# Causal masks on POOL in two instructions of two heads each, with a new instruction order, in a kernel of attention and token MLP

## The chip, the cores and the metric

One core of one Trainium2 chip. The metric is the device time of one execution in microseconds (us). The kernel before takes 174.0 us (median of 3 runs, 173.86 to 174.17). All times below are of fast runs, medians and ranges too; the slow are named and left out.

## The reference, cut to what matters

The output is a gated sum of two branches over X (2048 x 448): attention in 4 segments of 512 tokens with 16 heads of 28, causal inside a segment, with a memory matrix carried from segment to segment; and an MLP across tokens.

```python
mask = (ar[:, None] < ar[None, :]) * -1000000000.0       # causal, inside a segment
for s in range(N):                                        # N = 4 segments
    logits = einsum('bhqd,bhkd->bhqk', qs, ks) * scale + mask
    p = softmax(logits)
    a_dot = einsum('bhqk,bhkd->bhqd', p, vs)
    num = einsum('bhld,bhde->bhle', phi(qs), M)           # memory of earlier segments
    den = einsum('bhld,bhd->bhl', phi(qs), z)[..., None] + 1e-06
    outs.append(g * num / den + (1 - g) * a_dot)
    M = M + einsum('bhld,bhle->bhde', phi(ks), vs)
    z = z + einsum('bhld->bhd', phi(ks))
a = concat(outs) @ wo
b = gelu(layernorm(x)^T @ w1 + b1) @ w2 + b2
out = gate * a + (1 - gate) * b
```

## The kernel before

Work is recorded as named operations with what they read and write. A table ORDER then fixes, by hand or search, the sequence on each of the five engines; waits are derived from the reads and writes. The exponentials of one score fill (128 keys x 4 heads x 512 columns) go to one buffer `g`; POOL then zeroes the part above the diagonal in each 128-column block of it, all four heads at once:

```python
op("ACT", lambda e: e.activation(pslot(g), ps[:, 0:4, :], ACT.Exp, scale=SCALE), reads=R_bank[0:4],
   writes=[g.res], take=g, name=f"exp{p}_{f}", ...)
for x, j, c0, w in FILLS[f]:
    op("POOL", lambda e, c0=c0: e.affine_select(pslot(g)[:, :, c0 : c0 + 128], pslot(g)[:, :, c0 : c0 + 128],
                                                pattern=[[0, 4], [1, 128]], compare_op=ALU.is_ge, fill=0.0,
                                                base=0, channel_multiplier=-1),
       reads=[g.res], writes=[g.res], name=f"mask{p}_{f}_{j}", ...)
```

`g.res` is one tracked resource: whoever reads or writes any part of the buffer waits for the last writer of any part.

A full matmul (128 x 128 weights) may be issued whole or as four matmuls of 32 columns that run side by side. The second form is chosen where PE is already working in 32-column tiles, to save a change of form (name `mst`: the memory product, 64 matmuls of 32 x 32; `pv`: probabilities times V):

```python
def mm(e, out, w, x, split, **kw):
    if not split:
        return e.matmul(out, w, x, ...)
    for q in range(0, 128, 32):
        last = e.matmul(out[q : q + 32], w[:, q : q + 32], x, ...)
    return last
```

The loads of W1, W2 and Wo, the transposes of X and of the keys are all issued from one engine, SP, in the sequence of its row of ORDER. W1 comes in seven loads of 1 MB into a ring of three slots.

The softmax here doesn't subtract the row's maximum and nothing guards it: scores larger than these inputs give would overflow.

## Time and profile before

| | before |
|---|---|
| time, median of 3 | 174.0 us |
| span of the profiled execution | 170.9 us (that execution took 172.65 us) |
| PE / DVE / ACT / POOL busy | 166.1 / 144.2 / 127.0 / 68.6 us |
| masks | 64, 637 ns median |

PE is busy nearly throughout, so the time is that of PE: useful columns, about 0.1 us at each change of form, and halts. The lines that carry it stand in the prediction. One thing to keep in view: the profiled execution, at 172.65 us, was faster than each of the three timed ones, by 1.2 us and more.

### The profile page before, as it was taken

How to read it: one execution, taken by the hardware profiler on the slowest of the kernel's cores; microseconds unless marked ns; L12 is line 12 of the kernel's file. 1: busy time of each engine (PE TensorE's matmuls, PEld its weight loads, DVE VectorE, ACT ScalarE, POOL GpSimd, SP SyncE). 2: the span in 40 equal slices, each digit the busy share in tenths (PEclk: the TensorE clock that was granted, in tenths of full speed). 3: DMA queues.
4: the chain of work that ended last, by engine and by line, in shares of the span. 5: the costliest groups of instructions: out<-in, count | busy, mean ns of one | idle time of the engine just before them, and what ended most of it. 6: DMA issues, size and time to landing. Idle time of an engine off the chain costs nothing.

```text
span 170.9 us, 4757 instructions
## 1 busy us (share of the span) xinstructions
PE 166.1 (97%) x1953; PEld 80.0 (47%) x1960; DVE 144.2 (84%) x324; ACT 127.0 (74%) x154; POOL 68.6 (40%) x98
## 2 busy tenths in 40 slices
PE   7999999999999999999999999999999999999994
PEld 3444334444445443445454445444554455555552
DVE  2889999879897899899999999996898999977115
ACT  3469999898999999998999999989767786001000
POOL 8043285352635103384242461156826956150000
PEclk9999999999999999999999999999999999999999
DMA  5999994555563885299326000815920099735103
GB/s 176 293 207 337 293 292 99 109 152 148 127 176 69 125 226 130 50 275 229 76 77 186 0 11 21 227 42 47 252 78 29 14 245 293 211 94 171 57 0 107
DMA packets 49733, 24.57 MB, mean 144 GB/s; under 512 B 14240, under 2 KB 49472, under 8 KB 49712
## 3 DMA queue, kind: packets, MB, share of 16 engines
q1 hardware_dynamic: 49024, 23.70, 54.9%
q10 hardware_dynamic: 688, 0.57, 1.1%
q8 instruction: 15, 0.25, 0.6%
q14 instruction: 6, 0.05, 0.1%
HBM read 18.76 MB, written 2.36 MB: 124 GB/s over the span
## 4 chain that ended last, share of the span: by engine, by line
PE 82%; ACT 6%; DVE 4%; POOL 3%; DMA 2%; issue 2%; ACTq 0%
PE t L284 38%; PE t L711 20%; PE t L286 12%; PE t L973 6%; PE t L1011 4%; ACT t L982 3%; DMA t<-in_A_x_dram 2%; POOL t L985 2%; ACT t L1087 1%; POOL t L1042 1%; DVE t L1093 1%; DVE t L806 1%; DVE t L1095 1%; PE t L683 1%; ACT t L791 1%
## 5 line engine op out<-in xcount | busy, mean ns | idle before, releaser
L982 ACT ACTIVATE t<-t 128x2048 bf16<-128x2048 f32 x40 | 75.1, 1878 | 8.1 <-PE t L973 7.9
L284 PE MATMUL t<-t 128*128 128x448 bf16 (+2 forms) x404 | 78.5, 347 | 0.7 <-DVE t L793 0.4
L985 POOL TENSOR_SCALAR_AFFINE_SELECT t<-t 128x512 bf16<-128x512 bf16 x64 | 42.5, 683 | 48.3 <-ACT t L982 47.8
L284 PEld LDWEIGHTS t<-t 128*128 128x128 bf16 x411 | 37.8, 98 | 37.2 <-issue 4.4
L711 PE MATMUL t<-t 64*128 64x512 bf16 (+1 forms) x308 | 35.4, 367 | 0.5
L286 PE MATMUL t<-t 128*32 128x448 bf16 (+1 forms) x508 | 28.8, 354 | 0.0
L1042 POOL TENSOR_TENSOR t<-t 128x448 bf16<-128x448 f32 x12 | 15.6, 1305 | 23.6 <-DVE t L1038 6.8
L711 PEld LDWEIGHTS t<-t 64*128 64x128 bf16 x308 | 15.2, 94 | 17.9 <-PE t L711 3.2
L1118 DVE SCALAR_TENSOR_TENSOR t<-t 128x448 bf16<-128x448 f32 (+2 forms) x17 | 10.6, 643 | 9.3 <-PE t L284 8.6
L1067 ACT ACTIVATE t<-t 128x448 bf16<-128x448 f32 x10 | 7.2, 726 | 13.2 <-PE t L284 11.6
L286 PEld LDWEIGHTS t<-t 128*32 128x32 bf16 x508 | 12.3, 96 | 9.0 <-issue 1.9
L973 PE MATMUL t<-t 28*128 28x512 bf16 (+3 forms) x256 | 15.8, 301 | 0.3
L1048 DVE STREAM_TRANSPOSE t<-t 128x512 bf16<-128x512 bf16 x16 | 10.9, 691 | 1.1 <-POOL t L1042 1.1
L1011 PE MATMUL t<-t 128*32 128x512 bf16 (+3 forms) x256 | 11.5, 300 | 0.0
L916 DVE BATCH_NORM_STATS2 t<-t 128x6 f32<-128x448 bf16 x16 | 9.3, 607 | 2.6 <-DMA t<-in_A_x_dram 2.6
L973 PEld LDWEIGHTS t<-t 28*128 28x128 bf16 x256 | 4.5, 92 | 14.6 <-ACT t L982 7.1
L1027 DVE STREAM_TRANSPOSE t<-t 128x512 f32<-128x512 f32 x16 | 11.1, 698 | 0.2
L1025 DVE STREAM_TRANSPOSE t<-t 128x512 f32<-128x512 f32 x12 | 8.5, 712 | 2.3 <-PE t L284 0.9
L1095 DVE SCALAR_TENSOR_TENSOR t<-t 128x448 f32<-128x448 f32 x14 | 9.1, 646 | 1.0 <-ACT t L1090 0.9
L1100 DVE SCALAR_TENSOR_TENSOR t<-t 128x448 bf16<-128x448 f32 x14 | 8.9, 638 | 0.4 <-ACT t L1098 0.4
L1011 PEld LDWEIGHTS t<-t 128*32 128x32 bf16 x256 | 6.4, 96 | 5.8 <-issue 1.0
L1087 ACT ACTIVATE t<-t 128x448 f32<-128x448 f32 x14 | 8.6, 643 | 0.2 <-DVE t L1100 0.2
(73 smaller groups left out, 162.9 us busy)
## 6 DMA issues: line engine op xcount, KB each, us to landing
t<-in_B_w_dram SPq DMA_DIRECT2D x7, 1024.0 KB, 6.5
t<-in_B_w_dram SPq DMA_DIRECT2D x8, 896.0 KB, 5.9
out_dram<-t SPq DMA_DIRECT2D x15, 112.0 KB, 1.8
t<-in_A_x_dram SPq DMA_DIRECT2D x3, 448.0 KB, 4.4
t<-in_A_wo_dram SPq DMA_DIRECT2D x4, 98.0 KB
t<-in_A_wk_dram SPq DMA_DIRECT2D x1, 336.0 KB, 4.4
t<-in_A_wq_dram SPq DMA_DIRECT2D x1, 336.0 KB, 4.4
spare_heads<-t SPq DMA_DIRECT2D x8, 32.0 KB
```

The costliest lines, as they stand in the source:

```text
L284: return e.matmul(out, w, x, skip_group_check=True, **kw)
L286: last = e.matmul(out[q : q + 32], w[:, q : q + 32], x, skip_group_check=True, **kw)
L711: last = e.matmul(bank(o["b"])[:, 0 : o["n"]], o["w"](r, c), o["x"](r, c), start=first, stop=end, skip_group_check=True)
L973: last = e.matmul(bank(hl)[:, c0 : c0 + w], kT[r, hg, s * 512 + j * 128 : s * 512 + j * 128 + 128], qT[r, hg, s * 512 + 128 * j : s * 512 ...
L982: op("ACT", lambda e: e.activation(pslot(g), ps[:, 0:4, :], ACT.Exp, scale=SCALE), reads=R_bank[0:4], writes=[g.res], take=g, name=f"exp{p ...
L985: op("POOL", lambda e, c0=c0: e.affine_select(pslot(g)[:, :, c0 : c0 + 128], pslot(g)[:, :, c0 : c0 + 128], pattern=[[0, 4], [1, 128]], co ...
L1011: last = e.matmul(bank(cb)[32 * hl : 32 * hl + 32, 128 * j : 512], vaug[:, 4 * s + j, 32 * h : 32 * h + 32], pslot(P_fill[u // 2][f])[:, h ...
L1027: dv(lambda e: e.transpose(t2[:, 0, :], bank(cb)[:, 0:512]), [bres(cb)], [R_tt[tb][0]], "ta", 630, use=(cb,))
L1042: op("POOL", lambda e: e.tensor_tensor(o3, n3[0], n3[1], op=ALU.add), reads=R_tt[tb], writes=[R_ob[tb]], name=f"o{u}", cost=1280, port=Tru ...
L1048: dv(lambda e: e.transpose(oT[:, hg, s * 512 : s * 512 + 512], o), [R_ob[tb]], qres(hg, s), "ot", 635)
L1095: op("DVE", lambda e: e.scalar_tensor_tensor(gg[:, q, :], gg[:, q, :], 1.0, vh[:, q, :], op0=ALU.add, op1=ALU.mult), reads=[R_gg[q], R_vh[ ...
L1118: op("DVE", lambda e: e.scalar_tensor_tensor(outst[:, p, c0:c1], bank(b)[:, 0 : c1 - c0], omg[:, T : T + 1], ag(T)[:, c0:c1], op0=ALU.mult ...
```

## The change

Its likely intent: a DVE instruction that meets a mask waits for a shorter one (such meetings are shown in the prediction), and a product could be fed sooner. The masks are halved, and the whole ORDER table is made anew for that.

```diff
         for x, j, c0, w in FILLS[f]:
-            op("POOL", lambda e, c0=c0: e.affine_select(pslot(g)[:, :, c0 : c0 + 128], ...
-                                                        pattern=[[0, 4], [1, 128]], ...),
-               reads=[g.res], writes=[g.res], name=f"mask{p}_{f}_{j}", cost=590, port=True, prio=pr)
+            for k in range(2):
+                op("POOL", lambda e, c0=c0, k=k: e.affine_select(
+                    pslot(g)[:, 2 * k : 2 * k + 2, c0 : c0 + 128], ...
+                    pattern=[[0, 2], [1, 128]], ...),
+                   reads=[g.res], writes=[g.res], name=f"mask{p}_{f}_{j}_{k}", cost=377, port=True, prio=pr)
@@ ORDER, all five rows replaced; of SP only this excerpt @@
-        ldwo2 ldw1_3 tk0_3 tk0_2 ldw1_4 tk1_1 dtx3_1 dtx2_0 dtx2_1 tk1_0 ldw1_5 dtx3_0 ...
+        ldw1_3 tk0_3 tk0_2 dtx3_1 ldw1_4 ldwo2 dtx2_0 dtx3_0 tk1_1 ldwo3 ldw1_6 ldw1_5 ...
@@ of PE only the stretch around the memory product of segment 0 (mst0) @@
-        u5-12:2 u7-4 sc2_1 u7-5 u5-14 u7-6:3 pv2=7 u5-15 u6-5 u7-9 u6-6:3 u7-10 sc2_2 u6-9 mst0=7 u6-10:2 pv3=6 ...
+        u6-3 u5-14 u6-4:2 u5-15 u6-6:2 pv2=7 sc2_2 u7-8 u6-8 u7-9 mst0=7 u7-10:2 u6-9 u7-12 pv3=6 sc2_3 ...
```

`ldw1_4` is the fifth W1 load, `tk` a transpose of keys, `dtx` one of X, `u7-8` the ninth matmul of MLP tile 7.

## The prediction

> **What bounds the kernel now.** I read four views in this order: the busy shares with the forty slices, the chain that ended last, the order of PE's work in time, and the waits. The first two name the engine.
>
> ```profile
> PE 166.1 (97%) x1953; PEld 80.0 (47%) x1960; DVE 144.2 (84%) x324; ACT 127.0 (74%) x154; POOL 68.6 (40%) x98
> PE   7999999999999999999999999999999999999994
> POOL 8043285352635103384242461156826956150000
> PE 82%; ACT 6%; DVE 4%; POOL 3%; DMA 2%; issue 2%; ACTq 0%
> ```
>
> TensorE (PE) is busy in 166.1 of 170.9 us, and only the first and the last slice are below nine tenths. 82% of the chain is PE's own; POOL, where the change is made, has 3% of it. But a busy PE can still be badly used, so I looked at how long its pieces take on the chain, whose lines are start, duration, engine and line:
>
> ```profile
> 43.00 3.32 PE t L284 x17
> ...
> 90.94 5.03 PE t L284 x26
> ...
> 118.92 0.33 PE t L973 x8
> ...
> 141.90 1.51 PE t L286 x32
> ```
>
> L284 is a full 128-column matmul, L286 the same product cut into four 32-column matmuls that run side by side, L973 the scores (four row bands side by side), L711 the projections (two halves), L1011 the product of masked probabilities and V. From 17 to 26 full matmuls the piece grows by 5.03 - 3.32 = 1.71 us, 190 ns each; 17 of them should then take 3.23 us, so a piece pays 0.09 us once. The cut form takes 1.51 / 8 = 189 ns per group of four: it is as cheap as the full form. A scores piece takes 0.33 us for 512 columns in each band, the columns of one full matmul: about 0.12 us is paid once there too. So PE pays about 0.1 us at each change of form. I counted 86 such changes in the order of its instructions: some 9 us, the largest loss in the kernel.
>
> The rest is small. Setting starts of successive PE pieces against 190 ns per 448 columns, I find about 5.5 us of halts between the first projection and the end; some 2 us of them are the projections' own two-step accumulation (PE waiting for PE), and the longest single one is 0.54 us. Adding the first loads (PE's first data matmul stands at 3.9 us) and the last copy and store (from 168.5 us), that is all there is outside useful columns.
>
> Masks are the third group of the page:
>
> ```profile
> L985 POOL TENSOR_SCALAR_AFFINE_SELECT t<-t 128x512 bf16<-128x512 bf16 x64 | 42.5, 683 | 48.3 <-ACT t L982 47.8
> L985 POOL TENSOR_SCALAR_AFFINE_SELECT t<-t x64: 630/637/1296, 21.1 to 142.5; 128x512 bf16<-128x512 bf16 x64
> L595 POOL TENSOR_SCALAR_AFFINE_SELECT t<-t 128x128 bf16<-128x128 bf16 x1 | 0.3, 294 | 0.1
> PEld t L1011 <- POOL t L985: 0.9, 3, 0.4
> PEld t L973 <- ACT t L982: 7.1, 20, 0.6
> ```
>
> The first is the group (busy us, mean ns, then idle before it), the second its minimum, median and maximum, the third the same operation on 128 columns. POOL sat 47.8 us idle waiting for the exponentials (L982), and what waits for a mask is PE's weight load for L1011: 0.9 us in three waits, part of which lies beside running matmuls. PE also waits 7.1 us in twenty waits for exponentials, again ahead of weight loads.
>
> **What the Trainium skill says.** "TensorEngine Tiling (Array Packing)", section Key Properties, says that changing the tiling mode drains the engine; the trace agrees, with 0.09 to 0.12 us at each change. "GPSIMD Engine Reference", section 3.1 Elementwise, gives each POOL instruction a dispatch part besides a part by element, so two halves must cost more than one whole; the two sizes above agree, as worked out below. The same page, section 8 Key points, says that POOL shares its SBUF interfaces with VectorE (DVE) and contends with DVE instructions in a 2-port mode or with two SBUF inputs. The trace agrees: a mask takes 637 ns as a rule and up to 1296 ns where it meets such a DVE instruction, and the other way round:
>
> ```profile
> L1036 DVE TENSOR_SCALAR t<-t x12: 141/176/481, 65.9 to 147.2; 128x16 f32<-128x16 f32 x12
> L1040 DVE TENSOR_TENSOR t<-t x12: 611/618/873, 69.3 to 149.5; 128x448 f32<-128x448 f32 x12
> ```
>
> The long ones of both groups, 481 and 873 ns, lie beside a mask.
>
> **The change part by part.** The diff does two things: it halves the masks, and it replaces the hand-set order of all five engines. The second cannot be read from the few words of the title, so I compared the instruction orders.
>
> *Masks.* 64 of 128x512 become 128 of 128x256. Through 294 ns at 128 columns and 637 at 512: (637 - 294) / 384 = 0.89 ns per column, so 256 columns take 294 + 128 x 0.89 = 408 ns (an estimate). 128 x 408 = 52.2 us against 42.5, that is 9.7 us more on POOL. In the trace two masks in a row take 1.22 us, so the second starts some 50 ns before the first ends; a pair of halves is then ready after 408 - 50 + 408 = 766 ns where one whole took 637: each mask comes 0.13 us later. All PE instructions that read a mask still wait for both halves, so no consumer starts earlier. What it gives is a shorter hold: a DVE instruction that meets a mask waits at most about 0.4 us in place of 0.64.
>
> *Moves between engines.* Counted by line: DVE loses four of L1071 (717 ns), two of L1093 (670), one L697 (400), three pads of L655 (474, 210 and about 0.1 us): 5.4 us, and gains about 0.6 us in evacuations, net -4.8, to about 139 us. ACT takes the four evacuations of L1071 (726 ns), two of L1090 (645) and the L697 copy (594) and about nothing else: +4.2, to 131 us. The four evacuations go to the last stage, where ACT did 1.5 us in 27. POOL takes the three pads, at 400 ns for 224 columns and 0.89 ns for each further one 1.40 + 0.37 + 0.25 = 2.0 us. POOL ends at 68.6 + 9.7 + 2.0 = 80 us, 47%: not a bound.
>
> *PE.* Its columns are the same. Seven full matmuls become seven groups of four (411 to 404 full, 508 to 536 cut): 7 x (189 - 190), nothing. Changes of form go from 86 to 84: 2 x 0.11 = -0.2 us. This is the only term that surely lies on the path. The projections' waits for PE itself are 21 before and after.
>
> *Start.* The matmuls of V now all stand ahead of K's, so K's pad, for which PE's weight load waited 0.5 us and PE halted 0.2 us, is ready earlier: -0.2. Against it, Q's largest pad is now on POOL. Wq landed at 9.1 us; two fewer small loads stand before it now. 9.1 + 0.4 + 0.4 + 1.4 + 0.4 = 11.7 us at the latest, and PE comes to Q's projection near 11.4: 0 to +0.3. Together 0.
>
> *End.* Output products of the last four rows of tiles wait for all four transposes of DVE (L1048). Before, the last ended at 153.8 us, 9.9 us after the last L1011, and PE reached the first such product 0.9 us later. Now 43 matmuls of 190 ns and one of the memory product stand between: 8.4 us; by adding DVE's and POOL's durations in their new order I get 7.8 us. It fits, with 0.6 us to spare in place of 0.9: 0, at worst +0.5.
>
> *Sum.* -0.2 (changes of form) + 0 (start) + 0 (end) + what the middle's halts become. There are 3 to 3.5 us of them that an order could remove, and a new order makes others of the same kind. I take -0.3 for them, since the order was made anew for these mask durations and later masks are therefore probably planned for. 174.0 - 0.2 - 0.3 = 173.5.
>
> **The rivals.** *Later masks become waits of PE.* About 16 L1011 or memory products wait for masks. If each were exposed by its full 0.13 us, 16 x 0.13 = +2.1 us: 176. Against: only 0.9 us of weight-load waits name masks before, so most are early by more than 0.13 us. *DVE freed and POOL's hold shorter.* DVE gains 4.8 us by the moves and, at some eight meetings of about 0.25 us, up to 1 us by shorter holds. If DVE were the pace-setter this would be 3%: 168. Against: its chain share is 4%, and what it finishes earlier, PE cannot take earlier while it is full. *ACT becomes the pace-setter.* It was busy 44.6 of 46 us between 64 and 110 us; two more evacuations there, 1.3 us, could delay exponentials and so scores: up to +1.3, 175. For it: PE already halts behind an exponential twice, by 0.3 and 0.2 us. *The new order is simply tighter.* All 3.5 us of avoidable halts gone: 170.3, the only way to faster by 2%.
>
> **Range and chances.** The certain term is -0.2 us; start, end, masks and ACT can each give a few tenths up, the halts a little over one down. That makes 172.2 to 175.2 for 8 in 10. Faster by over 2% (under 170.5) needs every halt gone: 0.03. Slower by over 2% (over 177.5) needs the mask and ACT rivals together: 0.04. Within 2%: 0.93.
>
> **What would show it.** Mask halves of about 408 ns and POOL near 80 us show the mask step; a mask half of 350 ns or less would make the delay vanish. PE busy of 165 to 167 us with the same 190 ns per full matmul and 0.1 us per change show the PE step. Weight-load waits of L1011 for masks up to 2 us, hardly seen in PE's halts, would show that later masks are hidden; 3 us or more would show the first rival. DVE near 139 and ACT near 131 us show the moves. Proved wrong I would be by halts in PE's middle that sum to under 3 or over 8 us, by a gap before the last output products, or by a first score later than 16 us.

## The result, and the profile after

The changed kernel took 175.99 us (median of 4, 174.91 to 176.1) beside 173.93 us (median of 4, 173.6 to 174.17). Ratio 1.0106, 95% interval 1.0063 to 1.0149. A ratio is the mean time of one kernel's fast runs over that of the other's in the same rounds, so it is not quite the ratio of the medians quoted. It is slower, by 1%, and lies outside the predicted range. (A repeat, experiment 11, gave 1.0061 and 175.15 us, just inside that range.)

Busy shares, the slices of PE and POOL, and the chain of the changed kernel:

```profile
PE 167.2 (97%) x1981; PEld 80.6 (47%) x1981; DVE 140.7 (81%) x315; ACT 131.6 (76%) x160; POOL 81.7 (47%) x165
PE   7999999999997999999999999999999999999994
POOL 5094077464237501294751663099673969150000
PE 82%; DVE 9%; DMA 3%; issue 3%; ACT 1%; ACTq 1%
```

Loads moved between engines as counted: DVE 140.7, ACT 131.6, POOL 81.7. What is new is a 7 in PE's row at the thirteenth slice (52 to 56 us), where before there were only nines. The masks of the changed kernel (minimum, median, maximum in ns):

```profile
L994 POOL TENSOR_SCALAR_AFFINE_SELECT t<-t x128: 400/406/974, 21.8 to 146.2; 128x256 bf16<-128x256 bf16 x128
  PEld t L1020: 0.2, 1
```

A half takes 406 ns as a rule (408 was estimated), and what waits for a mask is a weight load (PEld), once, for 0.2 us, less than before. So masks are not what PE waits for. The hole in the slice is seen in PE's work in time (start, duration, line; line numbers above 1000 are 9 higher than before, so L1020 is the former L1011; the memory product is L858 before and L866 after), first of before, then of the changed kernel:

```profile
52.75 0.67 PE L858 MATMUL t<-t 128*32 128x32 bf16 x64
53.24 0.57 PE L286 MATMUL t<-t 128*32 128x448 bf16 x8
53.62 0.73 PE L1011 MATMUL t<-t 128*32 128x512 bf16 x16
```

```profile
52.36 0.75 PE L286 MATMUL t<-t 128*32 128x448 bf16 x12
53.02 0.66 PE L866 MATMUL t<-t 128*32 128x32 bf16 x64
53.50 0.56 PE L286 MATMUL t<-t 128*32 128x448 bf16 x6
55.13 0.74 PE L286 MATMUL t<-t 128*32 128x448 bf16 x10 [1.07 <-issue]
55.52 0.89 PE L1020 MATMUL t<-t 128*32 128x512 bf16 x16
```

PE stops in the middle of cut MLP matmuls, two parts into a group of four, for 1.07 us by modelled ends and 1.25 us by starts against the usual pace. The releaser is "issue": PE waited for nothing that the profile names. No semaphore instruction is recorded there either; the next one follows the halt, at 55.17 us. And the DMA share in those microseconds, first of before, then of the changed kernel (window, us, busy of PE, PEld, DVE, ACT, POOL with counts, clock, DMA share, GB/s; a packet's whole time is counted where it starts, so a share can exceed 1):

```profile
50.00:51.00 1.00, 1.00 (x36) 0.51 (x28) 0.97 (x3) 1.00 (x1) 0.18 (x1) 1.00 0.00 0
51.00:52.00 1.00, 1.00 (x28) 0.51 (x20) 1.00 (x2) 0.80 (x2) 0.59 (x2) 1.00 0.40 84
52.00:53.00 1.00, 1.00 (x55) 0.49 (x48) 0.33 (x2) 1.00 (x3) 1.00 (x3) 1.00 0.49 63
```

```profile
50.00:51.00 1.00, 1.00 (x24) 0.54 (x20) 0.86 (x3) 1.00 (x2) 0.08 (x1) 1.00 1.14 344
51.00:52.00 1.00, 1.00 (x28) 0.54 (x20) 1.00 (x3) 1.00 (x2) 0.06 (x1) 1.00 1.17 315
52.00:53.00 1.00, 1.00 (x28) 0.36 (x21) 0.97 (x3) 1.00 (x3) 1.00 (x3) 1.00 1.11 277
53.00:54.00 1.00, 1.00 (x74) 0.63 (x71) 0.93 (x4) 1.00 (x1) 0.57 (x2) 1.00 0.12 21
54.00:55.00 1.00, 0.06 (x2) 0.00 (x0) 1.00 (x3) 1.00 (x2) 0.26 (x1) 1.00 0.00 0
```

In the changed kernel the DMA engines are full from 50 to 53 us (a W1 load and, behind it, a Wo load), and PE stands still in the 55th microsecond although they are then idle. What links the two is in the DMA queues. The page lists a queue of kind "instruction" (packets, MB, share), before and after alike:

```profile
q8 instruction: 15, 0.25, 0.6%
```

Fifteen packets of 16,384 bytes spread over the whole execution, 5 to 15 us apart. The Trainium skill, "Perfetto Trace Analysis", section The 4-stage abstract model, says that instructions are of 64 bytes, so a packet is 256 of them; PE's stream has about 4,000 recorded instructions (1981 matmuls, as many weight loads, 64 semaphore instructions), 15 to 16 packets' worth. So q8 most likely carries PE's own instructions while it runs. Counting supports this: when PE's recorded instructions are cut into stretches of 256 (with one stretch ending at the 1217th, where PE stops), each packet starts in the next stretch in turn, 13 of 15 in the trace of before and 12 of 15 in that of the changed kernel exactly, the others within 34 instructions of it. One of the packets moved at 51.0 us before, and at 52.6 us in the changed kernel, behind the W1 load.

**Theory 1:** PE ran out of instructions. Its next 256 came late because a W1 load filled the DMA engines, and the memory product (64 matmuls and 64 weight loads in half a microsecond) with cut matmuls on both sides used up what it had. **Rivals:** the halves themselves cost the time; the halt is a hidden wait for a result, or chance; the later start (first score at 16.4 us in place of 15.8) comes from the new sequence of the first loads.

### The profile page after: what moved, and what is told of

The parts are those of the page before. It is cut to its first block, busy times and chain, and to the rows that moved or that the text cites.

```text
span 173.1 us, 4864 instructions
## 1 busy us (share of the span) xinstructions
PE 167.2 (97%) x1981; PEld 80.6 (47%) x1981; DVE 140.7 (81%) x315; ACT 131.6 (76%) x160; POOL 81.7 (47%) x165
## 4 chain that ended last, share of the span: by engine, by line
PE 82%; DVE 9%; DMA 3%; issue 3%; ACT 1%; ACTq 1%
PE t L284 40%; PE t L719 17%; PE t L286 13%; PE t L981 7%; PE t L1020 4%; DMA t<-in_A_wv_dram 3%; DVE t L1036 1%; DVE t L1109 1%; DVE t L1104 1%; DVE t L828 1%; DVE t L757 1%; ACT t L1099 1%; DVE t L1102 1%; DVE t L1057 1%; DVE t L803 1%
## 5 line engine op out<-in xcount | busy, mean ns | idle before, releaser
L994 POOL TENSOR_SCALAR_AFFINE_SELECT t<-t 128x256 bf16<-128x256 bf16 x128 | 56.2, 466 | 49.3 <-ACT t L990 47.3
L284 PE MATMUL t<-t 128*128 128x448 bf16 (+2 forms) x404 | 77.7, 347 | 0.0
L284 PEld LDWEIGHTS t<-t 128*128 128x128 bf16 x404 | 37.1, 98 | 36.1 <-issue 4.8
L286 PE MATMUL t<-t 128*32 128x448 bf16 (+1 forms) x536 | 30.6, 355 | 1.4 <-issue 1.1
L1051 POOL TENSOR_TENSOR t<-t 128x448 bf16<-128x448 f32 x12 | 13.6, 1138 | 16.6 <-DVE t L1047 10.1
L1076 ACT ACTIVATE t<-t 128x448 bf16<-128x448 f32 x14 | 10.1, 725 | 13.1 <-PE t L284 11.5
L286 PEld LDWEIGHTS t<-t 128*32 128x32 bf16 x536 | 12.8, 96 | 11.4 <-issue 3.3
L981 PE MATMUL t<-t 28*128 28x512 bf16 (+3 forms) x256 | 15.8, 301 | 0.1
L1020 PE MATMUL t<-t 128*32 128x256 bf16 (+3 forms) x256 | 11.7, 300 | 0.0
L1104 DVE SCALAR_TENSOR_TENSOR t<-t 128x448 f32<-128x448 f32 x14 | 9.3, 663 | 1.0 <-ACT t L1099 1.0
L1020 PEld LDWEIGHTS t<-t 128*32 128x32 bf16 x256 | 6.8, 97 | 5.5 <-issue 0.8
L1047 DVE SCALAR_TENSOR_TENSOR t<-t 128x448 f32<-128x448 f32 x12 | 8.7, 724 | 0.1
```

The costliest lines, as they stand in the source:

```text
L284: return e.matmul(out, w, x, skip_group_check=True, **kw)
L286: last = e.matmul(out[q : q + 32], w[:, q : q + 32], x, skip_group_check=True, **kw)
L981: last = e.matmul(bank(hl)[:, c0 : c0 + w], kT[r, hg, s * 512 + j * 128 : s * 512 + j * 128 + 128], qT[r, hg, s * 512 + 128 * j : s * 512 ...
L994: op("POOL", lambda e, c0=c0, k=k: e.affine_select(pslot(g)[:, 2 * k : 2 * k + 2, c0 : c0 + 128], pslot(g)[:, 2 * k : 2 * k + 2, c0 : c0 + ...
L1020: last = e.matmul(bank(cb)[32 * hl : 32 * hl + 32, 128 * j : 512], vaug[:, 4 * s + j, 32 * h : 32 * h + 32], pslot(P_fill[u // 2][f])[:, h ...
L1051: op("POOL", lambda e: e.tensor_tensor(o3, n3[0], n3[1], op=ALU.add), reads=R_tt[tb], writes=[R_ob[tb]], name=f"o{u}", cost=1280, port=Tru ...
```

## The experiments

Each kernel differs from before or from the changed kernel by the edit shown.

**1. Halves alone, in the old order.**

```diff
 ORDER["POOL"]:
-  mask0_1_1 maskg0 mask0_0_0 mask0_1_3 ...
+  mask0_1_1_0 mask0_1_1_1 maskg0 mask0_0_0_0 mask0_0_0_1 mask0_1_3_0 mask0_1_3_1 ...
```

> The order of before with each mask in two halves, standing next to each other on POOL. Theory (the new order, not the halves, costs the time): within 0.4 us of before, 173.6 to 174.4, with POOL near 78 us and PE's weight loads waiting for masks no more than 2 us. Rival (halves come later and PE waits for them): 175.5 or more, with a few us of waits of L1011 for masks.

177.16 us (176.94 to 179.11) beside 174.68; ratio 1.0177, interval 1.0091 to 1.0262. The theory missed: halves alone cost at least as much as the whole change. PE's own waits, in this kernel (L1012 is the product with V, L986 the mask):

```profile
PE t L1012 <- POOL t L986: 2.7, 5, 0.9
```

Five halts, 2.7 us, where PE itself (not just its weight loads) had none for masks before. POOL's work in time at the first of them, before and in this kernel:

```profile
24.22 1.34 POOL L985 TENSOR_SCALAR_AFFINE_SELECT t<-t 128x512 bf16<-128x512 bf16 x2 [0.61 <-ACT t L982]
```

```profile
23.54 3.51 POOL L986 TENSOR_SCALAR_AFFINE_SELECT t<-t 128x256 bf16<-128x256 bf16 x7
```

Seven halves take 3.51 us, 0.50 us each, so a mask costs POOL 1.0 us against 0.67 of the whole. Starts of successive undisturbed halves lie 0.36 us apart in some places and 0.47 to 0.48 in most: the second half waits for the first through `g.res`, though they touch different heads. So the change by itself is a loss, and the new order is what hides it: PE waited 2.7 us for halves in the old order, and none in the new one.

**2. The new order with whole masks.**

```diff
 ORDER["POOL"]:
-  mask0_1_1_0 mask0_1_1_1 mask0_0_0_0 maskg0 ...
+  mask0_1_1 mask0_0_0 maskg0 ...
```

> The order of the changed kernel with every mask whole again, at the place of its first half. Theory (the new order costs the time): 175 to 176.2, as slow as the changed kernel, and the halt of about 1.2 us in PE near 54 us, in cut matmuls just after the memory product of segment 0, is there again. Rival (the halves cost it): back to about 174, no halt.

175.09 us (174.75 to 175.74, and one slow run) beside 174.68; ratio 1.0039, interval 0.9956 to 1.0122. The halt is there:

```profile
PE t L286 <- issue: 0.9, 1, 0.9
```

1.1 us by starts, before the same instruction. So it belongs to the new order, not to the halves. The time alone does not tell: the interval holds both expectations. The trace does: from the first score to the last matmul it takes 154.8 us, with whole masks, where the changed kernel takes 154.1 and before 152.6 (a table below has this stretch for more runs).

**3. The W1 load issued later.**

```diff
 ORDER["SP"]:
-  tk0_3 tk0_2 dtx3_1 ldw1_4 ldwo2 dtx2_0 dtx3_0 tk1_1 ...
+  tk0_3 tk0_2 dtx3_1 dtx2_0 dtx3_0 ldw1_4 ldwo2 tk1_1 ...
```

> The changed kernel with one W1 load and one Wo load issued behind the two X transposes that followed them, on SP alone. Theory (PE ran out of instructions at 54 us, because its 16 KB instruction fetch was delayed by this W1 load, which filled the DMA engines from 49 to 53 us): the fetch moves from 52.6 to about 50 to 51 us, the halt of 1.2 us is gone or under 0.3 us, time 174.6 to 175.2. Rival (the halt is a wait for a result that the profile does not name, or chance): the halt stays, 175.5 to 176.2.

177.92 and 175.98 us (two more runs were slow) beside 174.68; ratio 1.014, interval 1.0019 to 1.0261. The packet moved to 50.7 us and the halt is gone, as expected. The time missed, for a reason of its own: the load was now too late for the MLP tile that reads it.

```profile
PE t L284 <- DMA t<-in_B_w_dram: 2.6, 1, 2.6
```

After that idle stretch eight matmuls took 300 to 374 ns each in place of 190 (the granted clock of that slice was 0.6). The load may neither fill the DMA engines while PE asks for instructions nor come late: that is why moving it is a poor repair.

**4. The first loads in the old sequence.**

```diff
 ORDER["SP"]:
-  ldx0 ldwv0 ldgw ldgwb ldwk ldwk0 ldwq ldwq0 ldx4 ldb2 dtx1_0 dtx1_1 ldx8 ldbeta ldb1 ldx12 ldw1_1 ldw1_0 ...
+  ldx0 ldwv0 ldgw ldgwb ldwk ldwk0 ldb1 ldbeta ldwq ldwq0 ldx4 dtx1_0 dtx1_1 ldb2 ldx8 ldx12 ldw1_0 ldw1_1 ...
```

> The changed kernel with the first loads issued in the order of before (the two small loads of b1 and beta ahead of Wq again), on SP alone. Theory (Wq's load, issued 0.85 us earlier, takes DMA share from X and Wv, so that PE starts 0.6 us later): first score from 16.4 back to about 15.8 us, time 175.2 to 175.6. Rival (the later start is chance of one execution): first score and time as the changed kernel's, 175.8 to 176.1.

175.81 us (175.65 to 175.89); ratio 1.0072, interval 0.9993 to 1.0151. The first score came at 16.6 us, no earlier. The rival holds: the start is chance. The halt was 2.0 us long this time.

**5. The kernel before once more.**

```diff
 (no edit)
```

> The kernel before, unchanged, profiled once more. Theory (its first profile was a lucky execution: 172.65 us against a median of 174.0): span 172 to 173 and the first score at 16.2 to 16.8 us in place of 15.8. Rival (the new order starts later by its nature): first score at 15.8 again.

173.59 us (one run, its state unknown), span 171.9 us, first score at 16.8 us, at the upper end of what was expected. The old order gave first scores from 15.8 to 17.8 us in five traces of it or of variants (17.8 where PE had waited 1.8 us for a load of X), the new order from 16.1 to 16.7 in nine. The 0.65 us of the first pair of traces is no property of the change.

**6. More matmuls in the cut form, to move the end of a block.** If a block of 256 instructions ends just behind the memory product, then 162 more instructions ahead of it put that end in front of the product. 27 full matmuls between 31 and 37 us are cut; no change of form is added, and SP is untouched.

```diff
+        for o in seq:
+            if o.name in ('u0-8', 'u0-9', 'u0-10', 'u1-8', ... 'u1-15', 'u3-5'):     # 27 names
+                o.alts = {"PE": (o.split,) + o.alts["PE"][1:]}
```

> The changed kernel with 27 full matmuls between 31 and 37 us put in the cut form, which adds 162 instructions to PE ahead of the memory product and no change of form. Theory (PE ran out of instructions where a block of 256 of them ends, just behind the memory product): the end of that block now falls ahead of the memory product, the halt of 1.2 to 2.0 us near 54 us is gone, 174.2 to 175.0. Rival (the halt belongs to that place or to those matmuls, not to the count of instructions): it stays, 175.6 to 176.2; cut matmuls cost something themselves: up to 0.3 us more.

173.81 us (173.66 to 175.13) beside 173.76; ratio 1.0015, interval 0.9964 to 1.0067. The halt is gone, though the DMA engines are as full as in the changed kernel; the times alone do not part the two (1.0061, 1.0017 to 1.0105, in experiment 11). The windows and PE's work of this kernel (its lines are 3 higher again):

```profile
50.00:51.00 1.00, 1.00 (x28) 0.48 (x24) 0.57 (x3) 1.00 (x2) 0.41 (x1) 1.00 1.13 344
51.00:52.00 1.00, 1.00 (x28) 0.56 (x24) 1.00 (x4) 1.00 (x1) 0.00 (x0) 1.00 1.19 313
52.00:53.00 1.00, 1.00 (x32) 0.50 (x28) 1.00 (x2) 1.00 (x3) 0.73 (x2) 1.00 1.15 286
```

```profile
53.35 0.66 PE L869 MATMUL t<-t 128*32 128x32 bf16 x64
53.83 0.95 PE L289 MATMUL t<-t 128*32 128x448 bf16 x16
54.59 0.73 PE L1023 MATMUL t<-t 128*32 128x512 bf16 x16
```

Same load, same memory product, same matmuls behind it, and they follow without a break. Only the count of instructions ahead differs, and with it the packets: they now move at 42.1 and 54.3 us, none between, so that the one of 52.6 us comes 10 us earlier. This is the experiment that decides for theory 1 against a hidden wait.

**7 and 8. Halves that do not wait for each other,** in the old and in the new order.

```diff
+        self.res2 = Res(pool + "2")          # each buffer: one resource per half
-                   reads=[g.res], writes=[g.res], name=f"mask{p}_{f}_{j}_{k}", ...
+                   reads=[(g.res, g.res2)[k]], writes=[(g.res, g.res2)[k]], name=f"mask{p}_{f}_{j}_{k}", ...
 # the exponential writes both; the products read both
```

> The order of before with halves, where the two halves of a mask no longer wait for each other on POOL (each half tracked by itself; both are disjoint). Theory (about half of the 2.5 us that halves cost in the old order comes from this wait, which spaced halves by 0.48 us where 0.36 are possible): 175.4 to 176.3, and PE's waits for masks 1.5 to 2.5 us in place of 3.6. Rival (collisions with DVE on the shared port are the cause): 176.7 to 177.3.

176.08 us (175.46 to 176.94) beside 173.76; ratio 1.0132, interval 1.0083 to 1.0181. All undisturbed halves are now 0.36 us apart, and PE's waits for them fell:

```profile
PE t L1013 <- POOL t L987: 1.5, 3, 1.0
```

By the times the self wait was about a quarter of the cost (1.0177 to 1.0132, but the intervals overlap); from the first score to the last matmul PE took 156.3 us with it and 154.8 without, where before took 152.6, so by the traces two fifths. What remains was not taken apart by a run; two things are seen: the second dispatch (2 x 0.36 against 0.59 us for the whole) and long halves, which in the first trace lay beside DVE instructions: 18 of 128 halves took over 450 ns there, their excess over the median 7.6 us in all, where of 64 whole masks 9 took over 700 ns with an excess of 3.0 us.

> The changed kernel, its halves likewise freed of waiting for each other. Theory (the new order already hides the masks: PE waited 0.2 us for them): 175.5 to 176.1, no gain, and the halt near 54 us is there. Rival (masks still delay it through POOL's other work): 175.2 or less.

174.9 us (174.49 to 175.69) beside 173.76; ratio 1.006, interval 1.0004 to 1.0116. Under the expected range and where the rival was put, but the halt is there with 1.65 us. One other wait vanished, PE's at 92 us for a DVE transpose, which the changed kernel has:

```profile
PE t L286 <- DVE t L1036: 0.3, 1, 0.3
```

By starts it is 0.46 us.

**9 and 10. Both repairs, and the new order repaired with whole masks.**

> The changed kernel with both repairs: 27 more matmuls in the cut form, so that no block of instructions ends behind the memory product, and halves that do not wait for each other. Theory (halt and self wait are separate losses; the second cost PE 0.45 us near 92 us): 173.0 to 173.6, at or a little under before. Rival (the second gain was chance of that chip): 173.6 to 174.2, as the first repair alone.

174.02 us (173.64 to 174.42, six runs) beside 173.85; ratio 1.0004, interval 0.9973 to 1.0035. Missed: the second repair adds nothing to the first that shows in the time, though its trace lacks the wait at 92 us; it has another, of 0.7 us for ACT at 19 us. Run beside experiment 11 on one chip, all six of its times (up to 174.42) lie under the three of the changed kernel (from 174.67).

> The new order with whole masks and 27 more cut matmuls. Theory (whole masks in the new order cost and gain little; the halt of 1.1 us goes): 174.0 to 174.6. Rival (the new order needs the halves): above 175.

173.58 us (173.39 to 174.92) beside 173.85; ratio 1.0001, interval 0.9949 to 1.0053. A little lower than expected. With the halt removed, the new order is as fast as the old one, with whole masks and with halves. No version here beats the kernel before by more than the noise.

**11. The changed kernel once more.**

> The changed kernel, unchanged, beside the others on one chip. Theory: ratio to before 1.008 to 1.012, and PE's halt of 1 to 2 us near 54 to 56 us is in its trace again, ending at the same instruction. Rival (the halt of the first trace was chance): no halt, ratio under 1.005.

175.15 us (174.67 to 175.22, and one slow run) beside 173.85; ratio 1.0061, interval 1.0017 to 1.0105, a little under the expected range. The halt is there (1.0 us by starts), before the same instruction.

**12. The halt made in the kernel before,** by DMA traffic alone.

```diff
+    side = nc.dram_tensor("side_copy", (S, 256), BF16, kind="Internal").ap()
+    op("SP", lambda e: e.dma_start(side, W1[:, 0:256]), writes=[R("side")], name="copy", dma=True, ...)
 ORDER["SP"]:
-  tk0_3 tk0_2 ldw1_4 tk1_1 ...
+  tk0_3 tk0_2 ldw1_4 copy tk1_1 ...
```

> The kernel before, with whole masks and the old order on every engine, and one more load on SP: 1 MB of W1 copied to an unused place in DRAM, issued just behind the W1 load at 44.3 us. Nothing reads the copy. Theory (DMA traffic that delays the instruction fetch is enough to halt PE behind the memory product): the fetch moves from about 51 to about 53 us and PE halts 0.8 to 2 us at 54 to 56 us, ended by nothing the profile names; time 1 to 2 us over before. Rival (the halt needs the new order): no halt, time within 0.4 us of before, or a wait named as DMA or transposed keys.

The packet moved from 51.0 to 53.25 us, and PE halted in a kernel of whole masks and old order (L1014 is the product with V):

```profile
54.34 0.54 PE L1014 MATMUL t<-t 128*32 128x512 bf16 x5
55.42 0.45 PE L1014 MATMUL t<-t 128*32 128x384 bf16 x8 [0.54 <-issue]
```

By starts it is 0.72 us, just under the expected 0.8. The time missed: 173.63 us (173.22 to 174.62, and one slow run) beside 173.62; ratio 0.9983, interval 0.9893 to 1.0072. A halt of 0.7 us, 0.4%, is within that interval, so the trace shows the halt and the time cannot show its cost. The trace also has a wait of 0.8 us at 104 us for a DMA (`spare_heads`), which the other traces lack and which was not followed up.

From the packet records of the traces: when the packet of q8 moved that comes next before the 1218th recorded instruction of PE, how many recorded instructions PE had begun by then, when the packet had landed, and when the 1218th began.

| trace | packet starts | PE's instructions begun | landed | 1218th begins | halt by starts |
|---|---|---|---|---|---|
| before | 51.02 | 1000 | 52.19 | 53.70 | none |
| before again | 52.19 | 1008 | 53.15 | 54.63 | none |
| halves, old order | 53.20 | 976 | 54.37 | 56.27 | none |
| W1 load later | 50.71 | 975 | 51.87 | 53.94 | none |
| changed kernel | 52.61 | 1071 | 53.79 | 55.13 | 1.25 us |
| changed kernel again | 52.24 | 1051 | 53.39 | 54.90 | 1.03 |
| new order, whole masks | 53.17 | 1055 | 54.53 | 55.79 | 1.11 |
| first loads old | 53.38 | 1138 | 54.69 | 56.05 | 2.01 |
| new order, no self wait | 53.29 | 1075 | 54.64 | 55.96 | 1.65 |
| before, side copy | 53.25 | 1053 | 54.21 | 55.43 | 0.72 |

Six halts, in two orders, with whole masks, with halves, and each ahead of the 1218th recorded instruction, which is an MLP matmul in the new order and one of the product with V in the old: 1217 and 63 more that are not recorded would be 5 x 256. PE resumes 1.2 to 1.5 us after the landing. A result waited for would not sit at the same count in different orders. The clock time of the packet does not decide: at 52.2 us it came in time in the second trace of before and late in the second of the changed kernel. What parts the two groups is how far PE had come: at most 1008 instructions, or at least 1051. The 256 recorded instructions ahead of the halt, the memory product among them, are begun within 3.2 to 3.5 us, and from a packet's start to PE's next instruction 2.2 to 2.7 us passed in the six halts. So even the kernel before had little to spare: its two packets landed 1.5 us before their first instruction was begun. That a block is fetched only shortly before it is needed, and that a load of 1 MB delays it (experiments 3 and 12, where SP's loads alone differ), is what the packet times show; how PE's sequencer decides to ask is not shown and stays open.

## Why the prediction was wrong, point by point

**What bounds the kernel, changes of form, columns, cut form:** right. Full matmuls stayed at 190 ns, changes of form at 0.1 us, PE's busy time was 167.2 us (165 to 167 foreseen). The cut form is as cheap per column as said, and 27 more of it cost nothing measurable. But it puts four times the instructions in the same time, and this cost has no line in the prediction.

**Masks:** the size of a half was right (406 ns for 408). POOL's total (81.7 us for 80) was right with luck: the masks came to 56.2 us in place of 52.2, because that sum left out the long ones, and 2.0 us less of products (15.6 to 13.6 us) made up for half of it. The delay of 0.13 us is what halves without a self wait show (2 x 0.36 - 0.59). With it the second half starts 0.47 to 0.48 us after the first, so a mask is ready some 0.24 us later in the old order; this dependence stands in the diff (`reads=[g.res], writes=[g.res]` for both halves) and was overlooked. The prediction also took the halves of a mask to stand side by side. In the changed kernel's order only 16 of 64 pairs do: from the start of a mask's first half to the end of its second 2.0 us pass (median), not 0.77. That masks are hidden was right for the new order (0.2 us of waits) and wrong for the old one, where "most are early by more than 0.13 us" failed: 2.7 us of PE's halts and 1.77%. The shorter hold did not pay: the excess of long halves more than doubled in total, 7.7 us in the changed kernel against 3.0 us on whole masks.

**Moves between engines:** right in kind (DVE 140.7 for 139, ACT 131.6 for 131); DVE lost 3.5 us and not 4.8.

**Start and end:** both given as 0, and so it was. The first score at 16.4 us, named as a sign of error, is chance: the kernel before shows 16.8. No gap came before the last output products. The other sign, PE's halts, would not have told either: those of over 0.1 us sum to 4.6 us in the changed kernel and 5.0 before, inside the 3 to 8 named.

**What the middle's halts become:** this step failed. "There are 3 to 3.5 us of them that an order could remove ... I take -0.3 for them." Two things were wrong. First, the 5.5 us held 1.3 us that were no halts: six steps of 0.22 us between full matmuls. They are memory products without a record, as the page of before shows when forms are kept apart, beside the page of the changed kernel:

```profile
L284 PE MATMUL t<-t 128*128 128x512 bf16 x1 | 0.4, 379 | 0.0
```

```profile
L284 PE MATMUL t<-t 128*128 128x512 bf16 x4 | 1.5, 379 | 0.0
```

The program of before issues eight such products (411 full matmuls in all, 404 recorded); one was recorded. In the changed kernel all four are. Second, the term had the wrong sign and size: in place of -0.3 us there is the instruction halt (1.0 to 2.0 us in five traces of the new order) and the wait of 0.46 us for DVE, so 1.7 and 1.5 us of new halts in the two traces of the changed kernel (1.25 + 0.46 and 1.03 + 0.46). The new order did remove halts, as was hoped: those of 0.54, 0.28 and 0.20 us between 54 and 62 us of before are gone, and smaller ones came elsewhere. The net is read from the first score to the last matmul, which leaves out the chance of the start:

| trace | from the first score to the last matmul |
|---|---|
| before, and again | 152.55, 152.43 us |
| changed kernel, and again | 154.05, 154.00 |
| experiments 6, 9, 10 (no instruction halt) | 152.88, 153.03, 152.91 |

So the stretch grew by 1.5 us where 0.5 less was foreseen (0.2 for changes of form, 0.3 here), and without the instruction halt 1.0 to 1.2 us of it are gone. The other 0.3 to 0.6 us were not taken apart; the wait for DVE is one part. In times, the ratios make it +1.8 us in the first comparison and +1.1 in the second.

**The rivals:** none of the four named an instruction fetch. That the first one's number, 176, is what was measured is a coincidence: its cause, waits for masks, came to 0.2 us. The range was cut to what waits of engines could do, and so was too narrow upward.

## What to carry to other kernels

Where PE is full, its instruction count is a resource like its columns: cutting a matmul in four is free in time and not in instructions, and a dense burst of small matmuls (256 instructions in 3.2 to 3.5 us here) behind a 1 MB load can leave PE without instructions. A halt named "issue" in the middle of a run, with full DMA just before, was the sign here; shifting the stream by some hundred instructions (162 here) is a cheap test and here the repair. The kernel before had no such halt, with 1.5 us from landing to need: so a new order could lose it by chance. Before halving an instruction on POOL, count the dispatch (a half takes POOL 0.36 us here, where half of a whole mask's 0.59 is 0.30), and give each half its own tracked resource, or the halves wait for each other.

## What the Trainium skill lacked or had wrong

- "Trainium Architecture — The Big Picture", section The software stack, says that the instruction streams are moved to each engine's memory when the program is loaded. Another page, "Runtime: NRT & Kernel Launch", section Instruction fetch mechanics, does describe a refill in blocks of 16 KiB, 256 instructions, while the engine runs, and calls its cost mostly hidden. Here 15 to 16 such packets move during the 171 to 176 us of the execution, and PE halted 0.7 to 2.0 us where one came late.
- No page gives the time from the landing of such a packet to PE's next instruction: 1.2 to 1.5 us in six traces; nor that other loads delay the packet: with a W1 load moving, PE had begun 1051 to 1138 recorded instructions when it started, and at most 1008 in four traces without.
- "TensorEngine Tiling (Array Packing)", section Key Properties, names the drain at a change of mode without a size: 0.09 to 0.12 us here, at some 86 places. The page does not say that column tiling multiplies the instructions: 256 of them took 3.2 to 3.5 us around the memory product.
- "GPSIMD Engine Reference", section 8 Key points, has the contention with DVE without a size: a 406 ns half took up to 974 ns in the changed kernel. No page gives the spacing of masks in a row: 0.59 us for 128 x 512, 0.36 for 128 x 256, 0.47 to 0.48 where the second waits for the first.
- "Perfetto Trace Analysis" does not warn that matmuls can lack a record: 7 of 1960 here in two traces of before, all memory products of 512 columns, which look like halts of 0.22 us.
